# K through a transposing DMA in place of PE transposes, in a two-layer GQA decode kernel

## The chip, the cores and the metric

The kernel runs on one core of a Trainium2 chip. The metric is the device time of one execution in microseconds (us), on the slowest core; with one core, that core. Three executions of the kernel before the change took 1404.67 to 1412.28 us, median 1409.17 us.

## The reference

The reference is two rounds of attention block and feed-forward block for 8 sequences, each decoding one token. Attention has 32 query heads over 8 KV heads, 8192 cached positions and a head size of 128.

```python
# x: [8, 1, 512]; k_cache, v_cache: [8, 8, 8192, 128], all bf16
q = (ln(x) @ wq) split into 32 heads
scores = einsum("bhqd,bhkd->bhqk", q, repeat(k_cache, 4)) * 128 ** -0.5
o = einsum("bhqk,bhkd->bhqd", softmax(scores), repeat(v_cache, 4))
x = x + o @ wo                      # twice in all, each followed by
x = x + silu(ln(x) @ w1) @ w2       # a small feed-forward block
```

There are 64 (batch, KV head) pairs per layer and two layers, so 128 pairs. Each pair brings 2 MiB of K and 2 MiB of V from HBM and uses them once. All else is small: about 20 MB of weights against 537 MB of K and V.

## The kernel before

The score matmul needs K with the head dimension on the partitions. So K is loaded as it lies, transposed by TensorE against an identity in blocks of 128 x 128, and copied from PSUM to SBUF by VectorE or ScalarE. For one pair that is 64 transposes and 8 copies.

```python
NKN, NKT, NV = 3, 2, 3            # tiles for K as loaded, K transposed, V
ACT_EVAC_GROUPS = (1, 4, 7)
...
def emit_kdma(j):                  # one 2 MiB load, 16 KB per partition
    src = A_k_cache[b, g].rearrange("(p c) d -> p c d", p=128)
    dma(sp, KNs[i], src, knsem[i], writes=[r_KN[i]])

def emit_vdma(j):
    src = A_v_cache[b, g].rearrange("(p c) d -> p c d", p=128)
    dma(sp, VSs[i], src, vsem[i], writes=[r_VS[i]])

def emit_tgroup(j, grp):           # 8 groups of 8 blocks
    for k in range(CPG):
        c = grp * CPG + k
        steps.append(lambda k=k, c=c: pe.transpose(tpv[:, k, :], KNs[kn][:, c, :], ident[:, :]))
    mm_group(steps, reads=[r_KN[kn], r_ident], writes=[r_TPp[tb]])
    if grp in ACT_EVAC_GROUPS:
        op(act, lambda: act.copy(dst, tpv), ...)
    else:
        op(dve, lambda: dve.tensor_copy(dst, tpv), ...)
...
# scores: K^T block is the stationary operand, 4 query columns move
pe.matmul(scp[:, c, :], KTs[kt][:, c, :], rhs, start=True, stop=True)
# PV: V block is stationary, 4 columns of probabilities move
pe.matmul(otp, VSs[vs][:, c, :], Ps[sl][:, :, c], start=(c == 0), stop=(c == NCH - 1))
...
for t in range(NPAIR + L_PV + 1):  # a software pipeline over the pairs
    jp = t - L_PV
    for grp in range(GROUPS):
        emit_tgroup(t + 1, grp); emit_scores_group(t, grp); emit_pv_group(jp, grp)
        # softmax of t - 1; norm of jp - 1, then the V load of jp - 1 + NV
    emit_kdma(t + 1 + NKN)
    if t == NPAIR // 2: load_wo()  # weights on the ACT queue
```

All K and V loads are issued by SP, in program order.

## Time and profile before

| | before |
|---|---|
| time, median of 3 | 1409.17 us |
| bytes moved, mean rate | 560.78 MB, 400 GB/s |
| DMA share and rate from 100 to 600 us | 1.01, 419 GB/s |
| TensorE busy | 1266.5 us (90%) |
| VectorE, ScalarE busy | 673.8 us, 450.6 us |
| spacing of SP's K issues | 10.25 us |

The page of the profile shows the busy time of the engines, then the DMA and rate in 40 slices of the span (a digit is the busy share in tenths), then the queues. Queue q1 carries what SP issues, q10 what ACT issues, and q8 is of the kind "instruction".

```profile
PE 1266.5 (90%) x25052; PEld 1235.7 (88%) x25052; DVE 673.8 (48%) x1436; ACT 450.6 (32%) x527; POOL 103.1 (7%) x263
DMA  9999999999999999999499999999999999999981
GB/s 390 395 399 409 420 419 424 425 425 411 421 420 419 418 420 406 425 419 416 161 419 377 427 426 416 416 413 413 409 421 419 420 420 418 423 423 425 422 367 64
q1 hardware_dynamic: 37440, 541.10, 92.1%
q8 instruction: 196, 3.21, 0.9%
```

The DMA row stands at 9 (90% or more) everywhere but at the layer boundary and the end. The windows view of 100 to 600 us says the same with one number; its last three columns are the granted TensorE clock, the DMA share and the rate.

```profile
core 0: us, PE busy (x) PEld busy (x) DVE busy (x) ACT busy (x) POOL busy (x), PEclk, DMA share, GB/s
100.00:600.00 500.00, 466.37 (x9228) 463.93 (x9225) 248.87 (x529) 163.79 (x193) 38.39 (x96) 0.59 1.01 419
```

TensorE is almost as full as the DMA (466 of 500 us), so the two limits lie close together. The chain of work that ended last therefore passes from one to the other (shares of the span by engine, then by line; L386 holds the transposes):

```profile
PE 61%; DMA 36%; issue 2%; DVE 0%; ACT 0%; SPq 0%; ACTq 0%; DVEq 0%
PE TPp L386 38%; DMA arena<-in_A_v_cache_dram 31%; PE OTp L495 12%; PE SCp L439 9%; DMA arena<-in_A_k_cache_dram 5%; PE MISC L544 1%; PE MISC L580 1%; DMA wreg<-in_A_wq_dram 1%; PE MISC L562 0%; DVE X L341 0%; ACT L311 0%; SPq L255 0%; ACT arena L391 0%; DVE xn L317 0%; DVE st_11 L307 0%
```

The costliest groups of instructions are the transposes, and the copies they need:

```profile
L386 PE MATMUL TPp<-ident,arena 128*128 128x128 bf16 x8192 | 937.6, 286 | 29.7 <-DMA arena<-in_A_k_cache_dram 19.0
L393 DVE COPY arena<-TPp 128x1024 bf16<-128x1024 bf16 x640 | 440.5, 691 | 505.1 <-PE TPp L386 498.8
L391 ACT COPY arena<-TPp 128x1024 bf16<-128x1024 bf16 x384 | 388.6, 1012 | 860.5 <-PE TPp L386 860.5
```

Last, the DMA issues of SP in order of time (start, length, engine, what). An issue is short, and a K and a V come every 10.25 us:

```profile
306.12 0.33 SPq L255 DMA_DIRECT2D arena<-in_A_k_cache_dram  x1
306.54 1.01 SPq L255 DMA_DIRECT2D arena<-in_A_v_cache_dram  x1
316.36 0.33 SPq L255 DMA_DIRECT2D arena<-in_A_k_cache_dram  x1
316.78 0.39 SPq L255 DMA_DIRECT2D arena<-in_A_v_cache_dram  x1
```

4.19 MB in 10.25 us is 409 GB/s. Both limits lie near there.

### The profile page before, as it was taken

The numbers are of one execution on the slowest core, as the hardware profiler recorded it, in microseconds if no ns is written. First come the engines' busy times: TensorE is split into PE (matmuls) and PEld (weight loads), VectorE is DVE, ScalarE is ACT, GpSimd is POOL, SyncE is SP. The second block draws the span as 40 slices with busy tenths as digits, with TensorE's granted clock in tenths as the row PEclk, the third lists the DMA queues.
The fourth block names the chain that finished last, engine by engine and source line by source line (L and its number), as shares of the span: only waits on it lengthen the run. The fifth ranks groups of instructions, "written<-read, shape, count | busy, mean of one in ns | idle before, by whom it ended". The sixth has DMA issues, their size and how long they took to land.

```text
span 1403.6 us, 53785 instructions
## 1 busy us (share of the span) xinstructions
PE 1266.5 (90%) x25052; PEld 1235.7 (88%) x25052; DVE 673.8 (48%) x1436; ACT 450.6 (32%) x527; POOL 103.1 (7%) x263
## 2 busy tenths in 40 slices
PE   3999999999987888998758899999999999888987
PEld 2999999999987888988538799999999999888984
DVE  1554544554544445555325455555555544445552
ACT  1433323333323323333124333333333333233331
POOL 0000000000000000000000000000000000000000
PEclk8655556555657667567767855555575555667677
DMA  9999999999999999999499999999999999999981
GB/s 390 395 399 409 420 419 424 425 425 411 421 420 419 418 420 406 425 419 416 161 419 377 427 426 416 416 413 413 409 421 419 420 420 418 423 423 425 422 367 64
DMA packets 48767, 560.78 MB, mean 400 GB/s; under 512 B 4240, under 2 KB 14240, under 8 KB 14752
## 3 DMA queue, kind: packets, MB, share of 16 engines
q1 hardware_dynamic: 37440, 541.10, 92.1%
q10 hardware_dynamic: 11104, 16.25, 3.2%
q8 instruction: 196, 3.21, 0.9%
q14 instruction: 27, 0.22, 0.0%
HBM read 557.33 MB, written 0.01 MB: 397 GB/s over the span
## 4 chain that ended last, share of the span: by engine, by line
PE 61%; DMA 36%; issue 2%; DVE 0%; ACT 0%; SPq 0%; ACTq 0%; DVEq 0%
PE TPp L386 38%; DMA arena<-in_A_v_cache_dram 31%; PE OTp L495 12%; PE SCp L439 9%; DMA arena<-in_A_k_cache_dram 5%; PE MISC L544 1%; PE MISC L580 1%; DMA wreg<-in_A_wq_dram 1%; PE MISC L562 0%; DVE X L341 0%; ACT L311 0%; SPq L255 0%; ACT arena L391 0%; DVE xn L317 0%; DVE st_11 L307 0%
## 5 line engine op out<-in xcount | busy, mean ns | idle before, releaser
L386 PE MATMUL TPp<-ident,arena 128*128 128x128 bf16 x8192 | 937.6, 286 | 29.7 <-DMA arena<-in_A_k_cache_dram 19.0
L386 PEld LDWEIGHTS TPp<-ident,arena 128*128 128x128 bf16 x8192 | 712.3, 129 | 30.6 <-DMA arena<-in_A_k_cache_dram 19.2
L393 DVE COPY arena<-TPp 128x1024 bf16<-128x1024 bf16 x640 | 440.5, 691 | 505.1 <-PE TPp L386 498.8
L391 ACT COPY arena<-TPp 128x1024 bf16<-128x1024 bf16 x384 | 388.6, 1012 | 860.5 <-PE TPp L386 860.5
L495 PE MATMUL OTp<-P,arena 128*128 128x4 bf16 x8192 | 366.4, 168 | 70.6 <-DMA arena<-in_A_v_cache_dram 61.7
L439 PEld LDWEIGHTS SCp<-QT,arena 128*128 128x128 bf16 x8192 | 398.4, 111 | 8.9 <-issue 7.4
L439 PE MATMUL SCp<-QT,arena 128*128 128x4 bf16 x8192 | 394.9, 170 | 6.1 <-issue 5.2
L495 PEld LDWEIGHTS OTp<-P,arena 128*128 128x128 bf16 x8192 | 295.8, 102 | 77.6 <-DMA arena<-in_A_v_cache_dram 66.0
L455 POOL PARTITION_ALL_REDUCE mxa<-mxp x128 | 47.4, 371 | 832.9 <-DVE mxp L450 832.9
L460 DVE TENSOR_TENSOR SCs<-SCs,mxa 128x256 f32<-128x256 f32 x128 | 54.5, 426 | 72.5 <-POOL mxa L455 72.5
L481 POOL PARTITION_ALL_REDUCE ssa<-ssm x128 | 55.0, 430 | 430.4 <-DVE ssm L476 430.4
L468 ACT ACTIVATE P<-SCs 128x256 bf16<-128x256 f32 x128 | 53.5, 418 | 31.3 <-DVE SCs L460 31.3
L484 DVE RECIPROCAL rcp<-ssa 128x4 f32<-128x4 f32 x128 | 22.8, 178 | 71.2 <-POOL ssa L481 71.2
L450 DVE TENSOR_REDUCE mxp<-SCs 128x4 f32<-128x256 f32 x128 | 53.8, 420 | 4.3
L447 DVE COPY SCs<-SCp 128x256 f32<-128x256 f32 x128 | 53.1, 415 | 3.2 <-PE SCp L439 3.2
L476 DVE TENSOR_REDUCE ssm<-P 128x4 f32<-128x256 bf16 x128 | 52.4, 409 | 1.6 <-ACT P L468 1.6
L507 DVE TENSOR_TENSOR attnT<-OTp,rcp 128x4 bf16<-128x4 f32 x128 | 21.3, 167 | 10.2 <-PE OTp L495 10.2
L544 PE MATMUL MISC<-wreg,attnT 128*8 128x512 bf16 x64 | 19.1, 472 | 0.5 <-DVE attnT L507 0.5
L326 PEld LDWEIGHTS MISC<-ident,xn 8*128 8x128 bf16 x16 | 0.7, 94 | 20.9 <-DVE xn L317 20.9
L326 PE MATMUL MISC<-ident,xn 8*128 8x8 bf16 x16 | 1.0, 165 | 19.5 <-DVE xn L317 19.5
L544 PEld LDWEIGHTS MISC<-wreg,attnT 128*8 128x8 bf16 x64 | 6.4, 102 | 12.4 <-issue 7.1
L341 DVE TENSOR_TENSOR X<-MISC,X 8x512 bf16<-8x512 f32 x4 | 2.7, 678 | 29.0 <-PE MISC L544 19.3
(26 smaller groups left out, 56.5 us busy)
## 6 DMA issues: line engine op xcount, KB each, us to landing
arena<-in_A_k_cache_dram SPq DMA_DIRECT2D x128, 2048.0 KB, 15.8
arena<-in_A_v_cache_dram SPq DMA_DIRECT2D x128, 2048.0 KB, 20.3
wreg<-in_A_wo_dram ACTq DMA_DIRECT2D x2, 4096.0 KB, 160.6
wreg<-in_A_wq_dram SPq DMA_DIRECT2D x2, 2048.0 KB, 7.5
wreg<-in_A_wq_dram ACTq DMA_DIRECT2D x2, 2048.0 KB, 19.6
w_5<-in_B_w_dram ACTq DMA_DIRECT2D x1, 1792.0 KB, 28.7
w_6<-in_B_w_dram ACTq DMA_DIRECT2D x1, 1792.0 KB, 96.1
X<-in_A_x_dram SPq DMA_DIRECT2D x1, 8.0 KB
```

What stands on the lines that cost most here:

```text
L386: lambda k=k, c=c: pe.transpose(tpv[:, k, :], KNs[kn][:, c, :], ident[:, :])
L391: op(act, lambda: act.copy(dst, tpv), reads=[r_TPp[tb]], writes=[r_KTg[kt][grp]])
L393: op(dve, lambda: dve.tensor_copy(dst, tpv), reads=[r_TPp[tb]], writes=[r_KTg[kt][grp]])
L439: lambda c=c: pe.matmul(scp[:, c, :], KTs[kt][:, c, :], rhs, start=True, stop=True)
L447: op(dve, lambda: dve.tensor_copy(SCs[sl][:, :, :], scp), reads=[r_SCp[bank]], writes=[r_SCs[sl]])
L450: lambda: dve.tensor_reduce(mxp[sl][:, :], SCs[sl][:, :, :], AX.X, ALU.max),
L455: lambda: pool.partition_all_reduce(mxa[sl][:, :], mxp[sl][:, :], 128, bass.bass_isa.ReduceOp.max),
L460: lambda: dve.tensor_tensor(SCs[sl][:, :, :], SCs[sl][:, :, :], mxa[sl][:, :].unsqueeze(2).to_broadcast([128, REP, NCH]), ALU.subtract,),
L468: lambda: act.activation(Ps[sl][:, :, :], SCs[sl][:, :, :], ACT.Exp, scale=SM_SCALE),
L476: lambda: dve.tensor_reduce(ssm[sl][:, :], Ps[sl][:, :, :], AX.X, ALU.add),
L481: lambda: pool.partition_all_reduce(ssa[sl][:, :], ssm[sl][:, :], 128, bass.bass_isa.ReduceOp.add),
L495: lambda c=c: pe.matmul(otp, VSs[vs][:, c, :], Ps[sl][:, :, c], start=(c == 0), stop=(c == NCH - 1))
```

## The change

The intent: let the DMA write K transposed, so that the 8192 transposes and their 1024 PSUM copies go away and TensorE, VectorE and ScalarE are freed.

```diff
-NKN = 3
-NKT = 2
+NKT = 4
-NTP = 3
-ACT_EVAC_GROUPS = (1, 4, 7)
...
                 def emit_kdma(j):
-                    i = kn_i(j)
+                    i = kt_i(j)
                     b, g = pair_bg(j)
-                    src = A_k_cache[b, g].rearrange("(p c) d -> p c d", p=128)
-                    dma(sp, KNs[i], src, knsem[i], writes=[r_KN[i]])
+                    src = A_k_cache[b, g].rearrange("(p c) d -> p (c d)", p=128)
+                    dma(sp, KTs[i], src, knsem[i], writes=[r_KT[i]], transpose=True)
...
-                def emit_tgroup(j, grp):
-                    ...                            # the whole function
...
                     for grp in range(GROUPS):
-                        if t + 1 < NPAIR:
-                            emit_tgroup(t + 1, grp)
                         if t < NPAIR:
                             emit_scores_group(t, grp)
...
-                    if t + 1 < NPAIR and t + 1 + NKN < NPAIR:
-                        emit_kdma(t + 1 + NKN)
+                    if t + NKT < NPAIR:
+                        emit_kdma(t + NKT)
```

The rest (tiles, PSUM banks and bookkeeping that are no longer needed) is cut here.

More of the change, by code (lines that the diff above doesn't have):

```diff
@@ L161, in ps_bank @@
         return ctx.enter_context(nc.psum_tensor(f"{name}_{_cnt[0]}", [128, n], dt))
-    NSLOTS = NKN + NKT + NV
+    NSLOTS = NKT + NV
     ARENA = sb([128, NSLOTS * SLOT], BF16, "arena")
@@ L167, in slot_ap @@
         return ARENA[:, i * SLOT:(i + 1) * SLOT]
-    KN_IDX = list(range(0, NKN))
-    KT_IDX = list(range(NKN, NKN + NKT))
-    V_IDX = list(range(NKN + NKT, NSLOTS))
+    KT_IDX = list(range(0, NKT))
+    V_IDX = list(range(NKT, NSLOTS))
     WREG = sb([128, max(WQ_ELEMS, WO_ELEMS)], BF16, "wreg")
@@ L174, in _build @@
     wo_sb = WREG[:, 0:WO_ELEMS].rearrange("p (h d) -> p h d", h=HQ)
-    KNs = [slot_ap(i).rearrange("p (c d) -> p c d", d=DH) for i in KN_IDX]
     KTs = [slot_ap(i).rearrange("p (c q) -> p c q", q=128) for i in KT_IDX]
@@ L204, in _build @@
     OTp = [ps_bank("OTp") for _ in range(2)]
-    TPp = [ps_bank("TPp", BF16) for _ in range(NTP)]
     MISC = ps_bank("MISC")
     syn = Sync(nc, ctx)
-    knsem = [DmaCounter(syn.new_sem(f"knsem{i}")) for i in range(NKN)]
+    knsem = [DmaCounter(syn.new_sem(f"knsem{i}")) for i in range(NKT)]
     vsem = [DmaCounter(syn.new_sem(f"vsem{i}")) for i in range(NV)]
@@ L221, in _build @@
     r_slot = [res(f"slot{i}") for i in range(NSLOTS)]
-    r_KN = [r_slot[i] for i in KN_IDX]
-    r_KTg = [[res(f"slot{i}_g{g}") for g in range(GROUPS)] for i in KT_IDX]
+    r_KT = [r_slot[i] for i in KT_IDX]
     r_VS = [r_slot[i] for i in V_IDX]
@@ L241, in _build @@
     r_OTp = [res(f"OTp{i}") for i in range(2)]
-    r_TPp = [res(f"TPp{i}") for i in range(NTP)]
     r_MISC = res("MISC")
@@ L292, in _ @@
             )
-            state = {"x": 0, "pair": 0, "tgroup": 0, "layer": 0}
+            state = {"x": 0, "pair": 0, "layer": 0}
             def load_wq():
@@ L350, in pair_bg @@
                     return j // HKV, j % HKV
-                def kn_i(j):
-                    return (base + j) % NKN
                 def kt_i(j):
@@ L374, in emit_vdma @@
                     dma(sp, VSs[i], src, vsem[i], writes=[r_VS[i]])
-                def emit_tgroup(j, grp):
-                    kn = kn_i(j)
-                    kt = kt_i(j)
-                    tb = state["tgroup"] % NTP
-                    state["tgroup"] += 1
-                    tpv = TPp[tb][:, :].rearrange("p (k q) -> p k q", q=128)
-                    steps = []
-                    for k in range(CPG):
-                        c = grp * CPG + k
-                        steps.append(
-                            lambda k=k, c=c: pe.transpose(tpv[:, k, :], KNs[kn][:, c, :], ident[:, :])
-                        )
-                    mm_group(steps, reads=[r_KN[kn], r_ident], writes=[r_TPp[tb]])
-                    dst = KTs[kt][:, grp * CPG:(grp + 1) * CPG, :]
-                    if grp in ACT_EVAC_GROUPS:
-                        op(act, lambda: act.copy(dst, tpv), reads=[r_TPp[tb]], writes=[r_KTg[kt][grp]])
-                    else:
-                        op(dve, lambda: dve.tensor_copy(dst, tpv), reads=[r_TPp[tb]], writes=[r_KTg[kt][grp]])
                 if first:
                     load_wq()
-                for j in range(max(NKN, NV)):
-                    if j < min(NKN, NPAIR):
+                for j in range(max(NKT, NV)):
+                    if j < min(NKT, NPAIR):
                         emit_kdma(j)
@@ L401, in attention_layer @@
                         emit_vdma(j)
-                for grp in range(GROUPS):
-                    emit_tgroup(0, grp)
-                if NKN < NPAIR:
-                    emit_kdma(NKN)
                 layernorm_and_transpose(xi)
@@ L440, in emit_scores_group @@
                         )
-                    mm_group(steps, reads=[r_KTg[kt][grp], r_QT], writes=[r_SCp[bank]])
+                    mm_group(steps, reads=[r_KT[kt], r_QT], writes=[r_SCp[bank]])
                 def emit_softmax_a(j):
```

## The prediction

It was written from the profile of the kernel before alone.

> **What bounds the kernel now.** Each of the 128 (batch, KV head) pairs brings 2 MiB of K and 2 MiB of V. The page's slices show the DMA engines at 9 (90% or more) nearly throughout; the windows view gives a DMA share of 1.00 and 415 to 425 GB/s between 200 and 1000 us. 560.78 MB at 420 GB/s is 1335 us of the 1403.6 us span; the other 69 us are start, layer boundary and tail. TensorE is almost equally full: 1266.5 us busy, 100% in the window 900:1000 at a granted clock of 0.50. Both limits lie at about 10.2 us per pair (SP's K issues are 10.25 us apart in the timeline), but DMA is the floor. The chain gives transposes 38% and V loads 31%; I read this as balance, not as a 38% prize.
>
> **What the change does.** It removes 8192 PE transposes (937.6 us busy; in the timeline some 0.73 us of each 1.28 us group, 5.8 us per pair), 640 DVE copies (440.5 us) and 384 ACT copies (388.6 us). TensorE keeps scores and PV: 0.55 us per group, 4.4 us per pair. DVE falls to some 235 us busy, ACT to 65. None of this lowers the DMA floor: the bytes are the same.
>
> It makes the 128 K loads transposing. Before, a K load took 2.097 MB / 420 GB/s = 5.0 us of all 16 engines. Its source has a 16 KB row pitch and is taken in 256-byte runs (128 bf16), so not contiguously. The Trainium skill, "DMA: Bandwidth & Descriptors", section "Latency and other measured facts", gives an effective 261 GB/s for a transpose with a non-contiguous mid-dim and about 350-400 for a contiguous one. This trace has no transpose. An estimate from that page: 2.097 MB / 261 = 8.0 us.
>
> K and V share the 16 engines, so the times add: 13.0 us per pair against 10.2.
>
> **Sum (estimate).** K 268.4 MB at 261 GB/s: 1028 us. V and weights, 292.4 MB at 420 GB/s: 696 us. Edges as before: 69 us. Total 1793 us. All of the added 3 us per pair is on the critical path, since DMA is already the bound; the removed PE work was hidden beside it. Four K tiles instead of three and two only change how far ahead loads run.
>
> At 375 GB/s the same sum is 1480 us, still slower. A transpose slower than 261, through the 16 KB pitch, or through holding SP so that V is issued late, would give 2000 to 2200 us.
>
> **Prediction: 1790 us, 8 in 10 between 1540 and 2200. Faster by over 2%: 6%; within 2%: 4%; slower by over 2%: 90%.**
>
> **What would show the steps right.** TensorE busy falls below 800 us, with waits on DMA the longest. The chain is nearly all DMA, with K first. The DMA stays busy in each slice while GB/s falls to about 320. K landing rises well over 8 us, and K issues are about 13 us apart. The K issue itself holds SP for microseconds (was 0.33 us).
>
> **What would make it wrong.** (a) Transposes at plain speed, or limited by something that V transfers overlap with: the period stays near 10 us, the time near 1409 or a little lower. (b) Transposes far below 261 GB/s: well over 2200 us. (c) Transposes and plain loads sharing the queue badly: DMA share would fall below 0.8, with SP waits or issue time in its place.

## The result, and the profile after

The changed kernel took 1972.08 us (median of 3, 1969.2 to 1974.2), against 1409.17 us. The ratio is 1.399, with a 95% interval of 1.390 to 1.408. A ratio here is the mean time of one kernel's fast runs over that of the other's fast runs of the same rounds, so it is not quite the ratio of the medians quoted beside it.

```profile
PE 515.0 (26%) x16860; PEld 479.8 (24%) x16860; DVE 262.5 (13%) x796; ACT 65.2 (3%) x142; POOL 103.2 (5%) x263
DMA  9999999999999999999799999999999999999994
GB/s 261 272 315 294 297 317 305 312 309 308 290 274 280 268 287 273 277 282 279 247 253 253 278 274 268 274 282 273 274 298 303 305 292 306 294 305 289 309 298 179
DMA packets 1082933, 559.66 MB, mean 284 GB/s; under 512 B 1054864, under 2 KB 1064864, under 8 KB 1065376
q1 hardware_dynamic: 1071680, 541.11, 109.6%
q8 instruction: 132, 2.16, 0.5%
HBM read 288.89 MB, written 0.01 MB: 146 GB/s over the span
```

TensorE fell from 1266.5 to 515.0 us busy, and VectorE from 673.8 to 262.5 us, as intended. The DMA row is still at 9 but for the layer boundary (7) and the end (4), while the rate fell from about 420 to between 247 and 317 GB/s. The same bytes now go in 1,054,864 packets under 512 bytes; 128 loads of 2 MiB in pieces of 256 bytes are 1,048,576 of them. Two warnings on reading these lines. A DMA share above 1 (109.6%) comes from packet records that overlap, so it is no measure of work done. And the HBM counter reads 288.89 MB, which is all traffic without the 268 MB of K: it does not see transposing reads.

```profile
100.00:600.00 500.00, 123.77 (x4352) 120.96 (x4352) 66.38 (x204) 14.15 (x34) 27.23 (x68) 1.00 1.18 301
```

Against the same window before, TensorE is at 124 in place of 466 us, and the rate at 301 in place of 419 GB/s. The chain is now:

```profile
SPq 95%; DMA 2%; PE 2%; issue 1%; DVE 0%; ACT 0%; DVEq 0%
SPq L247 94%; DMA arena<-in_A_v_cache_dram 2%; PE MISC L508 1%; PE OTp L461 1%; PE MISC L544 0%; SPq L71 0%; PE SCp L405 0%; PE MISC L526 0%; DVE X L333 0%; DVE st_11 L299 0%; DVE xn L309 0%; DVE attnT L473 0%; ACT sdv L303 0%; DVE hsT L537
```

It names SP's queue because the issue of a transposing load does not return for some 13 us, as the issues in order of time show:

```profile
312.62 0.52 SPq L247 DMA_DIRECT2D arena<-in_A_v_cache_dram  x1
313.68 13.02 SPq L247 DMA_TRANSPOSE arena<-in_A_k_cache_dram  x1
326.80 0.52 SPq L247 DMA_DIRECT2D arena<-in_A_v_cache_dram  x1
327.41 12.83 SPq L247 DMA_TRANSPOSE arena<-in_A_k_cache_dram  x1
```

An issue of K was 0.33 us and is now 13.02 us; the period is 13.6 us here and 15.2 us in the middle of the run. TensorE waits for V, 1315.1 us in all, which is the largest wait of the group that is now its costliest:

```profile
L461 PE MATMUL OTp<-P,arena 128*128 128x4 bf16 x8192 | 375.9, 169 | 1317.7 <-DMA arena<-in_A_v_cache_dram 1315.1
```

Is SP held because making a transpose takes SP that long, or because the 16 DMA engines are still busy with the V load before it? The page cannot tell; an experiment can. The view that tells most is the DMA in small slices. Here are 10 us of the changed kernel in 40 slices of 0.25 us:

```profile
GB/s 0 721 328 0 983 66 42 279 291 292 290 288 291 291 290 289 294 288 290 291 291 287 292 293 289 289 292 290 288 291 294 287 341 272 20 0 8 9 9 128
q8 instruction: 1, 0.02, 0.6%
```

In the first seven slices the last packets of V land (16 KB each, so their slices jump). Then K runs at 290 GB/s, flat within a few GB/s for more than 6 us. Then the rate falls to 20, 0, 8, 9, 9: for about 1.3 us almost nothing moves. In the window lies one packet of q8, the instruction queue, of 16 KB (0.02 MB). That gave two things to explain: the 290 GB/s, and the stop.

### The profile page after: what moved, and what is told of

Read it like the earlier page. It is cut to its first block, busy times and chain, and to the rows that moved or that the text cites. A ratio compares the mean times of both kernels' runs of the same rounds, so it can differ in the third digit from the quotient of the medians.

```text
span 1972.1 us, 36227 instructions
## 1 busy us (share of the span) xinstructions
PE 515.0 (26%) x16860; PEld 479.8 (24%) x16860; DVE 262.5 (13%) x796; ACT 65.2 (3%) x142; POOL 103.2 (5%) x263
## 2 busy tenths in 40 slices
DMA packets 1082933, 559.66 MB, mean 284 GB/s; under 512 B 1054864, under 2 KB 1064864, under 8 KB 1065376
## 3 DMA queue, kind: packets, MB, share of 16 engines
q1 hardware_dynamic: 1071680, 541.11, 109.6%
HBM read 288.89 MB, written 0.01 MB: 146 GB/s over the span
## 4 chain that ended last, share of the span: by engine, by line
SPq 95%; DMA 2%; PE 2%; issue 1%; DVE 0%; ACT 0%; DVEq 0%
SPq L247 94%; DMA arena<-in_A_v_cache_dram 2%; PE MISC L508 1%; PE OTp L461 1%; PE MISC L544 0%; SPq L71 0%; PE SCp L405 0%; PE MISC L526 0%; DVE X L333 0%; DVE st_11 L299 0%; DVE xn L309 0%; DVE attnT L473 0%; ACT sdv L303 0%; DVE hsT L537 0%; ACT sg L534 0%
## 5 line engine op out<-in xcount | busy, mean ns | idle before, releaser
L461 PE MATMUL OTp<-P,arena 128*128 128x4 bf16 x8192 | 375.9, 169 | 1317.7 <-DMA arena<-in_A_v_cache_dram 1315.1
L405 PE MATMUL SCp<-QT,arena 128*128 128x4 bf16 x8192 | 361.2, 166 | 90.6 <-DMA arena<-in_A_k_cache_dram 86.0
L405 PEld LDWEIGHTS SCp<-QT,arena 128*128 128x128 bf16 x8192 | 296.9, 104 | 93.8 <-DMA arena<-in_A_k_cache_dram 86.8
L379 PE MATMUL MISC<-xnT,wreg 128*128 128x8 bf16 x256 | 7.1, 168 | 16.4 <-DMA wreg<-in_A_wq_dram 16.4
L379 PEld LDWEIGHTS MISC<-xnT,wreg 128*128 128x128 bf16 x256 | 7.0, 104 | 16.6 <-DMA wreg<-in_A_wq_dram 16.6
L544 PE MATMUL MISC<-w_6,hsT 128*8 128x512 bf16 x28 | 10.3, 545 | 1.5 <-DVE hsT L537 1.5
## 6 DMA issues: line engine op xcount, KB each, us to landing
wreg<-in_A_wq_dram ACTq DMA_DIRECT2D x2, 2048.0 KB, 16.7
arena<-in_A_k_cache_dram SPq DMA_TRANSPOSE x128, 16.7
w_5<-in_B_w_dram ACTq DMA_DIRECT2D x1, 1792.0 KB, 13.9
```

The lines of the kernel that those rows point to most:

```text
L405: lambda c=c: pe.matmul(scp[:, c, :], KTs[kt][:, c, :], rhs, start=True, stop=True)
L461: lambda c=c: pe.matmul(otp, VSs[vs][:, c, :], Ps[sl][:, :, c], start=(c == 0), stop=(c == NCH - 1))
```

## The experiments

Twelve kernels were run. Where rounds were timed, each took its own runs of the kernel before on the same chip; their medians were 1410.75, 1411.56 and 1412.32 us in the three batches. Figures "by the records" below are worked out from the trace's record of each DMA packet. All the kernels passed the comparison with the reference, also those that are wrong: V and K act too weakly on the output for it. So the comparison says nothing of whether K and V are right, in the changed kernel too. By "crossbar" some expectations mean the transposing path of the DMA; what works inside it was not seen.

### k_only: the transposing loads without V

```diff
-                    dma(sp, VSs[i], src, vsem[i], writes=[r_VS[i]])
+                    if base == 0 and j < NV:
+                        dma(sp, VSs[i], src, vsem[i], writes=[r_VS[i]])
```

> Wrong result on purpose: V is loaded only for the first three pairs. Theory A (K and V take turns on the same 16 DMA engines, so their times add): SP is held 8 to 9.5 us per K issue, a period of 9 to 10 us, total 1200 to 1350 us, and 290 GB/s between stalls. Rival B (SP or descriptor generation needs about 12.9 us per transpose and V moves under it): the hold stays at 12.8 to 13 us and the total stays at 1700 us or more.

It took 1368.78 us (one run, so of unknown state). SP's K issues, merged by the view because nothing stands between them:

```profile
194.65 70.27 SPq L247 DMA_TRANSPOSE arena<-in_A_k_cache_dram  x8
```

That is 8.8 us per issue, against 12.9 with V. So 4.1 us of each hold were V's time on the DMA engines, and rival B, a fixed cost of SP, falls. Theory A was a little low: later in the run the issues are 10 us apart, and the total lies just above its range. The plain reading of the result is worth stating: about half of the traffic, transposing, takes 97% of the time that the kernel before needs for all of it. The stop is there without V too:

```profile
GB/s 288 290 291 293 286 292 293 288 290 291 290 289 291 294 287 291 291 290 341 273 84 2 7 10 9 171 290 279 289 312 390 210 355 367 352 384 335 390 342 370
q8 instruction: 1, 0.02, 0.6%
```

The rate goes 290, 84, 2, 7, 10, 9, 171, 290. (After that, wo loads beside K.) Of what is left, 8.8 us, 7.2 us are 2.097 MB at 290 GB/s and 1.6 us are mostly the stop.

### plain_k: the change without its transpose

```diff
-                    src = A_k_cache[b, g].rearrange("(p c) d -> p (c d)", p=128)
-                    dma(sp, KTs[i], src, knsem[i], writes=[r_KT[i]], transpose=True)
+                    src = A_k_cache[b, g].rearrange("(p c) d -> p c d", p=128)
+                    dma(sp, KTs[i], src, knsem[i], writes=[r_KT[i]])
```

> Wrong result on purpose: the changed kernel with plain K loads, 16 KB runs, no transpose anywhere. It is the change's removal of PE work without its transposing DMA. Theory (DMA is the floor of the kernel before, 560 MB at 420 GB/s, and the removed PE work was hidden): 1360 to 1405 us, 0 to 3% faster than before. Rival (TensorE, with the transposes at 38% of the chain, was the bound): below 1300 us is impossible at 420 GB/s, so the rival would show as a DMA rate well over 425 GB/s and under 1340 us.

It took 1381.28 us, ratio 0.979 (0.975 to 0.984) to the kernel before, which is inside the range expected. The gain is clear of noise; whether it is over 2% is not, as 2% lies in the interval. This splits the change in two. Taking all transposes and copies away, for nothing, is worth some 2.1%; making the loads transpose costs the 591 us from 1381.28 to 1972.08. The DMA rate between 200 and 600 us rises from about 419 to 424 GB/s:

```profile
200.00:600.00 400.00, 142.51 (x4999) 139.28 (x4996) 76.14 (x234) 16.23 (x39) 31.33 (x78) 1.00 1.01 424
```

So with these loads 1381 us is about the best that getting rid of the transposes could have reached: the DMA floor.

### contig: the source of each block in one piece

```diff
-                    src = A_k_cache[b, g].rearrange("(p c) d -> p (c d)", p=128)
-                    dma(sp, KTs[i], src, knsem[i], writes=[r_KT[i]], transpose=True)
+                    dma(sp, KTs[i], A_k_cache[b, g], knsem[i], writes=[r_KT[i]], transpose=True)
...
-KTs[kt][:, c, :]
+KTs[kt].rearrange("p (q c) -> p c q", q=128)[:, c, :]
```

> Right result: each block of 16 source rows is now one contiguous 4 KB, the 2 MiB of a pair are read in order, scores take strided columns instead. Theory C (the 16 KB row pitch is what holds K at 290 GB/s instead of 350 or more): steady K rate 350 to 400 GB/s, total 1700 to 1850 us. Rival D (256-byte packets, or the crossbar itself, set the rate): steady rate stays 285 to 295 GB/s and the total is within 2% of the changed kernel, 1930 to 2010 us.

It took 1925.71 us, ratio 1.365 (1.360 to 1.369). In slices of 0.2 us, the rate of K is:

```profile
GB/s 42 42 280 289 292 288 289 288 294 289 292 288 289 288 294 289 292 288 289 288 294 289 292 288 289 288 294 289 292 288 289 288 294 289 292 870 87 82 164 0
```

It is 290 GB/s again, so the row pitch of 16 KB is not what holds K down; theory C falls. The total is 2.4% below the changed kernel, just under rival D's range. TensorE's time also doubled (1022.5 us busy), where the only change to its work is that the stationary operand is read with a stride; this moves the instruction fetches to other places of the loads (by the records 0.77 per K load in place of 0.94). By the records its median period is 13.7 us in pairs 36 to 62, where the changed kernel has 15.2 (the uneven stretch below). Whether the places of the fetches gave the 46 us was not tested.

### plain_k256 and plain_k512: short runs without a transpose

```diff
 # plain_k256, against plain_k
-                    src = A_k_cache[b, g].rearrange("(p c) d -> p c d", p=128)
+                    src = A_k_cache[b, g].rearrange("(c p) d -> p c d", p=128)
 # plain_k512, against plain_k
+                    src = A_k_cache[b, g].rearrange("(c p k) d -> p c (k d)", p=128, k=2)
+                    dst = KTs[i].rearrange("p (c k) q -> p c (k q)", k=2)
```

> Wrong result on purpose: as plain_k, but K is fetched in 256-byte runs, the packet size of the transposing load, still without a transpose. Theory I (the packet size alone sets the 290 GB/s): K at 280 to 300 GB/s, total 1590 to 1680 us, and no stop of all engines at an instruction fetch. Rival J (the crossbar sets it): K at 380 GB/s or more, total 1370 to 1450 us.

> Wrong result on purpose: plain K loads in 512-byte runs. plain_k256 moved K at 218 GB/s, 18.8 ns per run and engine, of which 9.8 ns is the plain rate of 420 GB/s; a fixed 9 ns per run would give 287 GB/s here and 1600 to 1700 us. Rival (a step, full rate from 512 bytes on): K at 400 GB/s or more, 1380 to 1430 us.

plain_k256 took 2005.94 us (ratio 1.423), outside both ranges; plain_k512 took 1669.11 us (ratio 1.183), inside the first. A window inside a K load of each (last column GB/s):

```profile
307.00:314.00 7.00, 3.66 (x128) 3.58 (x128) 1.83 (x6) 0.42 (x1) 0.80 (x2) 1.00 1.11 218
```
```profile
304.00:308.00 4.00, 3.14 (x115) 3.05 (x112) 0.84 (x2) 0.00 (x0) 0.28 (x1) 1.00 1.08 298
```

At 218 GB/s, 16 engines move a run of 256 bytes in 18.8 ns each (16 x 256 / 218); at 298 GB/s, a run of 512 bytes in 27.5 ns; in plain_k a run of 16 KB goes at 424 GB/s, which is 9.7 ns per 256 bytes. (The 298 is one window; in slices of 0.5 us with K alone the median over the run is 291.) So each run costs 8 to 9 ns on top of its bytes. The transposing load takes 16 x 256 / 290 = 14.1 ns for its packets of 256 bytes. Rival J, that short runs would be fast without a transpose, falls. The profile writes these plain loads down in packets of four runs (1024 and 2048 bytes), so they match the transposing load in run length, not in packet size as the expectation has it. What the pair shows is that short runs alone bring a cost of this kind and that the transposing load is not slower than a plain load of the same run length. They do not show that both are slow for the same reason: the plain loads also read with other strides, and I had put the plain 256-byte load at 290 GB/s, not 218. Whether the engines or the making of descriptors set the 290 GB/s is open as well.

One part of theory I held: no stop at an instruction fetch. Here is such a load with a fetch packet, which starts in slice 21 (1330.06 us) and falls inside K:

```profile
GB/s 225 213 213 225 217 213 221 217 213 213 217 225 221 213 217 213 221 221 217 217 274 197 209 221 221 221 406 475 258 176 279 344 414 459 459 393 328 524 393 524
q8 instruction: 1, 0.02, 0.8%
```

By the records, around the 15 fetches with only K's packets from 1 us before to 1.5 us after their start, the median rate stays between 205 and 233 GB/s. So the stop does not come with short runs as such.

plain_k256 also shows that a held queue is no mark of a transpose. Here the issue of V, plain, stands behind K's short runs for 14.49 us:

```profile
299.56 14.49 SPq L247 DMA_DIRECT2D arena<-in_A_v_cache_dram  x1
314.27 0.71 SPq L247 DMA_DIRECT2D arena<-in_A_k_cache_dram  x1
```

### scores_x3, few_pv and few_mm: more and fewer instruction fetches

TensorE's 256 instructions per pair (a weight load and a matmul for each of 64 + 64) fill one q8 packet of 16 KB. The Trainium skill, "Runtime: NRT & Kernel Launch", section "Instruction fetch mechanics", says that instructions are fetched in 16 KiB blocks of 256, and that crossing a block boundary is mostly hidden. The counts agree: 33,720 TensorE instructions of the changed kernel / 256 = 131.7, and q8 has 132 packets.

```diff
 # scores_x3
-                    mm_group(steps, reads=[r_KT[kt], r_QT], writes=[r_SCp[bank]])
+                    mm_group(steps * 3, reads=[r_KT[kt], r_QT], writes=[r_SCp[bank]])
 # few_pv: in the PV group;   few_mm: in the PV and the scores group
-                    for k in range(CPG):
+                    for k in range(0, CPG, 7):
 # few_mm also clears the two scores banks once, as most of them is no longer written
```

> Right result: every scores matmul is done three times, TensorE stays below 60% busy. It doubles TensorE's instructions per pair, from 256 to 512, so two 16 KB instruction-fetch packets per pair in place of one. Theory E (each fetch packet stops all transposing engines for 1.5 to 2.5 us): +190 to +320 us, total 2160 to 2290 us. Rival F (the stop near the end of each K load has another cause and only coincides with the fetch): total within 2% of 1972 us, one stop per K load as before.

> Wrong result on purpose: 16 of the 64 PV matmuls per pair are left, so 160 TensorE instructions per pair and 0.63 instruction-fetch packets in place of 1.0. Theory E (a fetch packet stops the transposing engines): K loads without a packet in or just before them take 7.2 to 7.6 us, those with one 8.6 to 9.9 us; total 50 to 110 us less than the changed kernel, 1860 to 1925 us. Rival F (the stop belongs to the K load itself): all K loads alike, total within 1% of 1972 us.

> Wrong result on purpose: 16 of 64 scores matmuls and 16 of 64 PV matmuls per pair, 64 TensorE instructions, a quarter of a fetch packet per pair. Theory E, in proportion (few_pv lost 76 us for 48 packets fewer, scores_x3 gained 137 us for 128 more, so 1.1 to 1.6 us a packet): another 48 packets fewer than few_pv, 1810 to 1850 us. Rival F (what few_pv saved came from the PV work, not from the fetches): 1880 us or more.

```profile
q8 instruction: 260, 4.26, 0.8%
```
```profile
q8 instruction: 84, 1.38, 0.3%
```
```profile
q8 instruction: 36, 0.59, 0.1%
```

| kernel | fetch packets | us | against the changed kernel | per packet |
|---|---|---|---|---|
| scores_x3 | 260 | 2108.67 | +137 | 1.07 |
| changed kernel | 132 | 1972.08 | | |
| few_pv | 84 | 1895.55 | -77 | 1.6 |
| few_mm | 36 | 1864.20 | -108 | 1.1 |

(Ratios to the kernel before: 1.494, 1.399, 1.344, 1.322.) The time rises with the packets in both directions, while TensorE stays below half of the span, so rival F falls. The size was overstated for scores_x3 (+190 expected), and few_mm lies between the two ranges, above E's. Part of that is seen in where a packet falls: by the records scores_x3 has 1.5 of its 2 packets per pair inside K loads, the rest fall into V. The comparison inside one run is cleaner: in few_mm, by the records and after the first 12 pairs, K loads with no fetch packet in or just before them took 7.96 us (median of 83), those with one 9.25 us (28); in few_pv 7.86 (42) and 9.18 us (69). So one fetch costs a K load 1.3 us. (The 7.2 to 7.6 us expected without one was too low. The five loads beside weights are left out.)

The stops also account for the totals. By the records, in slices of 0.1 us, K loads stand under 50 GB/s for 300 us in scores_x3, 175 in the changed kernel, 103 in few_pv and 63 in few_mm. The differences to the changed kernel are +125, -72 and -112 us, close to the +137, -77 and -108 us of the totals.

The direct view agrees. By the records, around the 113 fetches of the changed kernel from 150 us after its first DMA packet to 150 us before its last, the median rate in steps of 0.25 us is 290, then from the start of the packet 272, 228, 16, 0, 5, 9, 10, 60, then 291. Around the same fetches in the kernel before (159) and in plain_k (107) there is no dip. So while one such packet is in flight, about 1.1 us, the transposing load stops nearly altogether; plain loads go on, those in short runs (plain_k256) too.

### w_on_sp and wo_at_end: the uneven stretch

By the records, the changed kernel's period (start of one K load to the next, median) is 13.6 us from pair 12 on (counted from 0), 15.2 us from about pair 36 to 92, and 14.2 us after that. The first change comes near the load of wo at pair 32.

```diff
 # w_on_sp: all four weight loads
-                dma(act, ...)
+                dma(sp, ...)
 # wo_at_end
-                    if t == NPAIR // 2:
-                        load_wo()
 ...
+                load_wo()
                 state["pair"] = base + NPAIR
```

> Right result: all weight loads move from the ACT queue to the SP queue, so nothing but instruction fetches runs beside a transpose. Theory G (a weight load that runs beside a transpose leaves the 16 engines out of step, which makes the stretch between the two wo loads slow, 15.2 us per pair against 14.1 before and after): every pair at 13.6 to 14.1 us, total 1860 to 1910 us. Rival H (the slow stretch comes from data addresses or from the chip): the stretch stays, total 1950 to 1990 us.

> Right result: wo is loaded after the last pair of each layer, not in the middle, so that nothing disturbs the queues at pair 32. Theory G2 (the wo load turns the even stretch of 13.6 us per pair into the uneven one of 15.2 us): pairs 36 to 62 stay at 13.5 to 14.0 us, total 1880 to 1950 us. Rival H (something else turns it, for example where the fetch falls): the uneven stretch starts near pair 34 all the same, total 1970 to 2000 us.

w_on_sp took 1960.36 us (ratio 1.388) and wo_at_end 1959.09 us (1.391). By the records the stretch is in both: 15.5 and 14.9 us per pair from 36 to 62, and it ends at pair 93 or 94 as before. In wo_at_end it starts at pair 38, with no weight load anywhere near. So theories G and G2 fall. w_on_sp's total is in the range of rival H; wo_at_end's total is outside both of its ranges, but its periods are those of rival H. What the stretch looks like is seen best in k_only, in slices of 0.25 us:

```profile
GB/s 291 291 288 293 289 290 321 9 0 4 9 9 12 283 289 291 291 289 290 293 290 170 95 244 221 188 169 232 220 238 194 188 85 137 290 292 289 290 291 291
```

Beside the stop of the fetch (9, 0, 4, 9, 9, 12) there is a second, softer slump of some 3.5 us, between 85 and 244 GB/s, where one K load follows another. In k_only, where no V can be involved, a K load spends by the records 1.0 us at between 50 and 275 GB/s in pairs 12 to 32 and 3.1 us in pairs 38 to 61, and 1.3 and 1.5 us at a standstill. What starts the slump is open. It ends where a second fetch packet falls into one K load (pair 92, in all three kernels), after which the fetches come at the ends of the loads; that is a coincidence seen three times, not a tested cause. Against the 13.6 us before it, it adds 1.6 us in some 57 of 128 pairs, about 90 us.

Two kernels narrow this down. few_pv and few_mm load the same weights and have no such stretch: by the records their median periods are 13.8 and 13.5 us in pairs 36 to 62, and 13.4 to 13.9 us in the others. So the stretch was seen only where about every K load holds a fetch. In the even pairs 12 to 31 of the changed kernel a fetch in each load costs the period little (13.6 us against 13.4 in few_mm for pairs without one), as the gap to the next K load, in which V runs, is then 0.5 us shorter. What a fetch costs is therefore no fixed sum; the 1.3 us is what it adds to the K load.

### v_on_act: V from another queue

```diff
-                    dma(sp, VSs[i], src, vsem[i], writes=[r_VS[i]])
+                    dma(act, VSs[i], src, vsem[i], writes=[r_VS[i]])
```

> Right result: V is issued from ACT, K stays on SP, so V no longer waits for SP to come free of a transpose and both kinds are in flight together. Theory A (the 16 engines are the limit, and a long plain packet on one engine stops the transpose on all): no gain, 1950 us or more, K's steady rate of 290 GB/s seen only where no V packet is in flight. Rival B2 (SP's hold, which puts K and V in single file, is the limit): V moves under K, period 12.2 us or less, total under 1800 us.

Its four runs took 1968.94 to 2086.39 us; three, with the profiled one, count as slow, so there is no ratio. The one fast run, 1968.94 us, is within 0.2% of the changed kernel, where rival B2 wanted under 1800. No run comes near 1800, so the single file on SP's queue was not what cost the time. The total fits theory A, as far as one fast run shows; its second half, when K runs at 290 GB/s, was not checked. The Trainium skill says so in general: "DMA: Bandwidth & Descriptors", section "Rules for kernel authors", holds that spreading DMAs over issuing engines for bandwidth does not help. The total of this run agrees. The profile of the slow run also holds a stretch near its end where K falls below 100 GB/s with V packets in between; as no fast run was profiled, nothing is concluded from it.

### wq_on_act: an edit to the kernel before

```diff
-                dma(sp, wq_sb[:, 0:half, :], src[:, 0:half, :], wsem["wq"], writes=r_wq)
+                dma(act, wq_sb[:, 0:half, :], src[:, 0:half, :], wsem["wq"], writes=r_wq)
```

> Right result: the kernel before with one edit, both halves of wq on the ACT queue. At the layer boundary SP stands 24 us before the second wq load, so the K and V loads of the second layer come late (one slice of 161 GB/s). Theory: they now start some 15 to 25 us earlier, 1385 to 1400 us, 0.7 to 1.8% faster than before. Rival: wq itself is then late behind the prefetched K and V and the start of the layer waits for it instead, within 0.5% of before.

This was a try at a version faster than both: the layer boundary is, but for the end, the one slice where the kernel before leaves much of the DMA idle. It took 1418.62 us, ratio 1.005 (1.002 to 1.009), so no faster, and at the edge of the rival's 0.5%. As the rival said, wq then comes late: ACT waited 35.5 us for it at the boundary, against 24.2 us in the kernel before. No run beat the kernel before with a usable result; plain_k, which did by 2.1%, computes the wrong scores.

## Why the prediction was right, and where it was off

**The bound.** "DMA is the floor" was right, and plain_k shows it: without any transpose work the time falls by only 2.1%. The prediction put this gain at zero; it is some 30 us against the kernel before of the same rounds.

**What falls away.** TensorE below 800 us (515.0), VectorE about 235 (262.5), ScalarE 65 (65.2): right within 12%.

**K and V share the engines, so their times add.** Right. k_only's hold of 8.8 us against 12.9 with V shows the sharing, and no run of v_on_act got round it by another queue.

**The size of the K term.** This is the term that was mis-sized: "K 268.4 MB at 261 GB/s: 1028 us". By the records, the 128 K loads of the changed kernel, each from first to last packet, add up to 1228 us, which is 219 GB/s (up to 48 us of it is for the 20 MB of weights that moved in between). The rest of the sum, 696 + 69 = 765 us, came out as 1972 - 1228 = 744 us. So K is 200 us over its term and the rest 21 us under; together they make the miss of 179 us. The number taken for K stands for several things that the prediction did not keep apart: a steady rate that is better than 261 GB/s (290), and stops and slumps that it did not foresee. That these came out near 261 together, and the total inside the range, is in part luck.

| per pair, us | plain_k | changed kernel | from |
|---|---|---|---|
| K, undisturbed | 5.0 | 7.2 | 2.097 MB at 424 and at 290 GB/s |
| V, undisturbed | 5.0 | 5.0 | 2.097 MB at 420 GB/s |
| taking turns, uneven starts, no fetch | | 1.2 | few_mm: loads of 7.96 and gaps of 5.5 us, less the two rows above |
| one instruction fetch | | 1.3 | few_pv and few_mm, loads with and without |
| sum | 10.0 | 14.7 | |

The sum is of typical parts; at 14.7 us it is inside the 13.6 to 15.2 us of the run. Over 128 pairs the steady rate gives (7.23 - 4.95) x 128 = 292 us of the 591 us between plain_k and the changed kernel, and the stops of the K loads 175 us. The remaining 124 us are taking turns, weights beside K and the slump of the uneven stretch; how they divide is open.

**The reason given for a slow transpose.** The prediction said "its source has a 16 KB row pitch ... so not contiguously" and took the slower of two figures for that reason. contig refutes it: the steady rate is 290 GB/s either way, above the one figure and below the other. What sets the 290 GB/s is open.

**The risk named.** "Through holding SP so that V is issued late" was the prediction's way to 2000 to 2200 us. SP was held for 13 us, but v_on_act speaks against the hold as what cost the time: it is the time of the DMA, seen from SP. The DMA stayed full and the rate fell, to 284 GB/s on average where "about 320" stood; K issues are 13.6 to 15.2 us apart where "about 13" stood. K landing "well over 8 us" was no test: its median is 16.7 us, but it was 15.8 us before. "The chain is nearly all DMA, with K first" was met only in substance: the profile writes it down as SP's queue, 95%, and the longest wait of TensorE is for V, because V stands behind K.

## What to carry to other kernels

Ask first which limit the freed work was under: here the transposes held 38% of the chain and were worth 2.1%, since the DMA was full beside them. Here a load that transposes cost the DMA more than a plain one of long runs (290 against 420 GB/s), so moving a transpose there can only pay where the DMA has time to spare. If transposing loads must run, count the instruction fetches beside them, and look at the DMA in slices of a quarter of a microsecond: the average hid a steady rate and a full stop.

## What the Trainium skill lacked or had wrong

- "Advanced Engine Details and Errata", section "X-Bar Transpose (TRN2)", says that transposing DMAs are as fast as regular ones and expects 350 to 400 GB/s. Here the steady rate was 290 GB/s, 69% of the 420 GB/s of plain loads, and 219 GB/s with its stops.
- "DMA: Bandwidth & Descriptors", section "Latency and other measured facts", gives 261 GB/s where a middle dimension is not contiguous and 350-400 for the contiguous case. A source in 256-byte rows at a pitch of 16 KB and one in order both ran at 290 GB/s.
- The same page, "Specifications", gives 512 B as the least transfer for line rate. Plain loads in runs of 512 bytes ran at 291 to 298 GB/s, of 256 bytes at 218, of 16 KB at 424.
- "Runtime: NRT & Kernel Launch", section "Instruction fetch mechanics", calls the cost of crossing a block boundary mostly hidden. Beside plain loads no stop was seen; beside a transposing load the DMA all but stopped for about 1.3 us, and the whole run changed by 1.1 to 1.6 us for each packet. No page has this.
- No page says how long a load of short runs, transposing or plain, holds the queue that issues it or the next load (12.9 us a transposing K behind V, 8.8 us without V, 14.5 us a plain V behind 256-byte runs; 0.33 us before), or that the profile's HBM counter leaves transposing reads out (288.89 MB counted, 557.33 MB before).
